# Lightning attention and a mixture of experts on one core: q and k turned in token halves on the two row halves of the array

## The chip, the cores and the metric

The kernel runs on one core of a Trainium2 chip. Its matrix engine (TensorE, "PE" in the profile, with the loading of stationary operands shown apart as "PEld") writes to PSUM banks of 128 partitions by 512 fp32 numbers. VectorE (DVE) and ScalarE (ACT) bring the results from there into SBUF, GpSimd (POOL) works on SBUF alone, and SyncE (SP) and ScalarE issue the DMAs. The metric is the device time of one execution in microseconds (us); less is better.

## The reference

Four batches of eight heads, 768 tokens and 64 numbers per head go through a decayed linear attention; its output, seen as 3072 tokens of 512, goes through four experts whose results are summed with normalised weights. All data are fp32.

```python
for b in range(nb):                                  # blocks of 64 tokens
    intra = einsum('bhic,bhjc->bhij', qb, kb) * Dmask[None]
    intra = einsum('bhij,bhjd->bhid', intra, vb)
    inter = einsum('bhid,bhde->bhie', qb * lam_pow[None], kv_state)
    out[:, :, sl] = intra + inter
    kv_state = lam_block[None, :, None, None] * kv_state + einsum('bhsd,bhse->bhde', kb * rev_pow[None], vb)
...
for e in range(E):                                   # x: (3072, 512), w1: (4, 512, 1024), w2: (4, 1024, 512)
    h = maximum(x @ w1[e], 0.0)
    out += p[:, e:e + 1] * (h @ w2[e])
```

## The kernel before

The tokens are worked on in three groups of 1024. The attention runs in chunks of 128 tokens rather than 64: eight chunks per group, 24 in all, numbered n. The expert products of a group are done by a seven-product scheme in place of eight (M1 to M7), on two levels, so that the operands are sums and differences of blocks, prepared by GpSimd and VectorE and stored by DMA for later use.

The order of all instructions is written by hand: each engine runs its instructions in the order in which the program issues them, and semaphores make an instruction wait for the data and the buffers of others.

A chunk of attention has three steps.

- `turn(n)` (line 420) brings q and k of the chunk from "tokens on partitions" to "head dimension on partitions". The natural tile `qn` holds, for each of four numbers `ac`, two heads side by side (128 columns). TensorE transposes those 128 x 128 blocks one by one: the block of data is the stationary operand and the identity matrix is the moving one. The four blocks of q fill one PSUM bank (`qp`), the four of k another (`kp`). ScalarE copies each bank as a whole, 128 x 512, to `qT` (line 431) and `kT` (line 432). VectorE then makes `qs`, the decayed q, and GpSimd multiplies `kn` by its decay in place, which has to wait until the transposes of k have read it.
- `scores(n)` (line 443) multiplies kT with qT (line 449): each head lies on 64 partitions, so each of these matmuls uses 64 of the 128 rows of the array, and two heads lie in the two halves. They write to two banks, one for each half.
- `values(n)` (line 461) multiplies the masked scores with v (line 477), adds what comes from the state (line 472), and forms the update of the state (line 485). The matmuls of line 485 have 64 columns of stationary operand and 64 of moving data, and alternate between the two column halves of the array.

One fp32 matmul in the program is two MATMUL instructions in the profile, each with its own LDWEIGHTS; a transpose is one.

The first group's attention (chunks 0 to 7, the loop at line 984) is done at the start, with pieces of the first expert products (line 955) put between its steps; there the banks come from three pairs, `pairs[n % 3]`. The 16 other chunks are spread over the expert products of the groups before them: `attention(g)` (line 504) makes a list of steps, and the main loop (line 1035) takes a step after some of its pieces. The banks are then `s0` and `s1`. Around each step lie matmuls of the first product (line 693) and of the second (line 747), with 128 x 128 stationary blocks and 256 moving columns.

The first product writes in turn to two banks, `g1` and `g3`; ScalarE copies (line 701) or VectorE adds (line 699) each result out before TensorE may write to that bank again.

`load(n)` (line 99) issues the DMAs for q and k (line 110) and v (line 106) on SyncE's queue. The stores of prepared weights (lines 148 to 150) are issued on ScalarE's queue, between its computing instructions.

Of the kernel before, what the change touches and what calls it, by code (L numbers as in the profile page):

```python
# [21 lines left out]
def kernel(  # L22
# [30 lines left out]
    nc = tc.nc  # L53

    B, H, S, D = q.shape
# [3 lines left out]
    C = P  # L59
    NHP = H // 2  # L60
# [21 lines left out]
    half = [slice(0, D), slice(D, P)]  # L82
# [4 lines left out]
    def bank(tag, name):  # L87
        return ps.tile([P, W], FP32, name=name, tag=tag)

    def small(name):  # L90
        return pool.tile([P, W], FP32, name=name, tag="t")

    def tt(eng, o, a, b, op):
        eng.tensor_tensor(out=o, in0=a, in1=b, op=op)  # L94
# [204 lines left out]
    ident = consts.tile([P, P], FP32, name="ident")  # L299
# [41 lines left out]
    for r in range(2):  # L341
        for ac in range(NHP):
            h = 4 * r + ac
            nc.vector.tensor_tensor_scan(
                out=s_decay[:, r, ac], data0=lam_bc[:, h:h + 1].to_broadcast([P, C]), data1=ident[:],
# [10 lines left out]
    while m < C:  # L356
        nc.vector.tensor_tensor(
            out=q_decay[:, :, m:2 * m], in0=q_decay[:, :, 0:m],
# [32 lines left out]
    def hc(t):  # L391
        return t[:].rearrange("p (h c) -> p h c", c=C)
# [21 lines left out]
    def soon(n, *work):  # L414

        background[0:0] = work
        if n < CPG:
            rest(len(work))

    def turn(n, tags):  # L420
        qn, kn = nat.pop((n, "q")), nat[n, "k"]
        qp = bank(tags[0], "qp")
        kp = bank(tags[1], "kp")
        for x, y in ((qp, qn), (kp, kn)):
            for ac in range(NHP):
                nc.tensor.transpose(  # L426
                    out=x[:, ac * C:(ac + 1) * C], in_=y[:, 2 * ac:2 * ac + 2].rearrange("p r d -> p (r d)"),
                    identity=ident[:],
                )
        qT, kT, qs = small("qT"), small("kT"), None  # L430
        nc.scalar.copy(out=qT[:], in_=qp[:])
        nc.scalar.copy(out=kT[:], in_=kp[:])
        if n % NCH:
            qs = small("qs")
            soon(n, lambda: tt(nc.vector, qs[:], qT[:], q_decay[:].rearrange("p h c -> p (h c)"), ALU.mult))
        turned[n] = qT, kT, qs
        if n % NCH < NCH - 1:

            kd = kn.rearrange("p (ac r) d -> p ac r d", r=2)
            by = k_decay.rearrange("p r ac -> p ac r").unsqueeze(3)  # L440
            tt(nc.gpsimd, kd, kd, by.to_broadcast([P, NHP, 2, D]), ALU.mult)
# [62 lines left out]
    def attention(g):  # L504

        steps = []
        early, late = prepare_x(g)
        for n in range(g * CPG, (g + 1) * CPG):
            steps.append(lambda n=n: turn(n, ("s0", "s1")))
            steps.append(lambda n=n: scores(n, ("s0", "s1")))  # L510

            def end(n=n):
                values(n, ("s0", "s1"))
                if n + AHEAD < B * NCH:
                    load(n + AHEAD)
                if n == g * CPG + CPG // 2 - 1:
                    chores.extend(early)
                if n == g * CPG + CPG - 1:
                    chores.extend(late)
            steps.append(end)  # L520
        return steps
# [462 lines left out]
    for i in range(CPG + 2):  # L984
        if i == 4:
            sum_w1(0, "S1", "A21", "A22", ALU.add)
            sum_w1(0, "S3", "A11", "A21", ALU.subtract)
        if i == 5:
            sum_w1(0, "S2", "S1", "A11", ALU.subtract)
            sum_w1(0, "S4", "A12", "S2", ALU.subtract)  # L990
            chores.extend(prepare_w2(0))
        if i > 5:
            pump()
        more = list(between.get(i, ()))
        for f, lag in ((scores, 1), (turn, 0), (values, 2)):
            n = i - lag
            if 0 <= n < CPG:
                f(n, pairs[n % 3])
            if i == 9 and lag == 2:
                x_sums()  # L1000
            if more:
                more.pop(0)()
        if i + 4 < CPG:
            load(i + 4)
        if i == 5:
            nc.scalar.dma_start(out=probs[:], in_=moe_domain_probs.rearrange("(t p) e -> p t e", p=P))
        if i == 9:
            gates()
# [26 lines left out]
    for at, (g, e) in enumerate(units):  # L1035
# [14 lines left out]
        for i in range(7):  # L1050
# [7 lines left out]
            if nests and i == 2:  # L1058
                nc.scalar.dma_start(
                    out=gate_bc[:], in_=gate_rows[:, ahead[1]].partition_broadcast(P),  # L1060
# [20 lines left out]
            for x, part in enumerate(order):  # L1081
# [12 lines left out]
                if turned_back and x > 0:  # L1094
                    y = turned_back.pop(0)
# [40 lines left out]
```

## Time and profile before

| | |
|---|---|
| median of 4 runs | 1220.06 us (1217.4 to 1221.35) |
| the profiled execution, its own time | 1220.19 us |
| its span in the profile | 1218.4 us |
| mean granted TensorE clock | 0.997 |
| transposes of line 426 | 96 for q and 96 for k |
| copies of lines 431 and 432 | 24 of 583 ns mean and 24 of 592 ns mean |
| HBM traffic | 233.49 MB read, 85.34 MB written |

The span runs from the first to the last instruction in the profile; 1.8 us of the execution's own time lie around it. In a row of the timeline the columns are the start in us, the length in us, the engine, the line, the operation, and what is written from what; shapes are given as stationary rows*columns, then the moving operand, and "x8" says that eight instructions in a row were merged. Matmuls overlap in the pipeline, so the pace of TensorE is read from start to start and not from the lengths.

### The profile page before, as it was taken

How to read it: one execution, taken by the hardware profiler on the slowest of the kernel's cores; microseconds unless marked ns; L12 is line 12 of the kernel's file. 1: busy time of each engine (PE TensorE's matmuls, PEld its weight loads, DVE VectorE, ACT ScalarE, POOL GpSimd, SP SyncE). 2: the span in 40 equal slices, each digit the busy share in tenths (PEclk: the TensorE clock that was granted, in tenths of full speed). 3: DMA queues.
4: the chain of work that ended last, by engine and by line, in shares of the span. 5: the costliest groups of instructions: out<-in, count | busy, mean ns of one | idle time of the engine just before them, and what ended most of it. 6: DMA issues, size and time to landing. Idle time of an engine off the chain costs nothing.

```text
span 1218.4 us, 17839 instructions
## 1 busy us (share of the span) xinstructions
PE 1194.1 (98%) x6621; PEld 1031.6 (85%) x6621; DVE 780.8 (64%) x1292; ACT 260.5 (21%) x476; POOL 627.1 (51%) x552
## 2 busy tenths in 40 slices
PE   6999998999999999999999999999999999999998
PEld 5888887888888888888888888888888888888877
DVE  5586575477466846746674874774665666777774
ACT  3322121112202211221221120120142241231132
POOL 3520265572382865025425746405675674873873
PEclk9999999999999999999999999999999999999999
DMA  9752679999899699889967999958966657565542
GB/s 227 194 170 108 215 264 336 343 345 316 303 340 341 231 326 368 265 274 293 312 224 266 287 336 351 306 220 299 347 252 220 250 194 275 194 259 210 205 171 72
DMA packets 228534, 320.03 MB, mean 263 GB/s; under 512 B 91712, under 2 KB 168928, under 8 KB 228448
## 3 DMA queue, kind: packets, MB, share of 16 engines
q1 hardware_dynamic: 157984, 233.47, 57.5%
q10 hardware_dynamic: 70464, 85.42, 19.5%
q8 instruction: 52, 0.85, 0.3%
q14 instruction: 34, 0.28, 0.1%
HBM read 233.49 MB, written 85.34 MB: 262 GB/s over the span
## 4 chain that ended last, share of the span: by engine, by line
PE 91%; DVE 3%; DMA 2%; SPq 2%; POOL 1%; issue 1%; ACT 0%; ACTq 0%; POOLq 0%; DVEq 0%
PE pg L693 34%; PE q L747 29%; PE pq L918 13%; PE pM L955 7%; PE op L477 2%; PE sp L449 2%; DVE hS L94 1%; POOL ops L94 1%; PE op L472 1%; DMA w_ops<-ops 1%; SPq L110 1%; DMA w2t<-w_sums 1%; PE qp L426 1%; PE kp L426 1%; DVE m L94 1%; PE op L485 1%
## 5 line engine op out<-in xcount | busy, mean ns | idle before, releaser
L693 PE MATMUL pg<-xs_in,ws_in 128*128 128x256 f32 x1960 | 475.3, 383 | 6.3 <-ACT m L701 4.4
L693 PEld LDWEIGHTS pg<-xs_in,ws_in 128*128 128x128 f32 x1960 | 368.6, 190 | 65.3 <-DVE m L94 8.1
L94 DVE TENSOR_TENSOR m<-pg,m 128x512 f32<-128x512 f32 x410 | 280.3, 689 | 130.2 <-PE pg L693 113.4
L747 PE MATMUL q<-w2t,hS 128*128 128x256 f32 x1024 | 242.5, 380 | 0.0
L747 PEld LDWEIGHTS q<-w2t,hS 128*128 128x128 f32 x1024 | 193.9, 190 | 26.7
L763 DVE SCALAR_TENSOR_TENSOR acc<-q,gate,acc 128x256 f32<-128x256 f32 x192 | 92.6, 482 | 152.8 <-PE q L747 152.5
L747 PE MATMUL q<-w2t,m 128*128 128x256 f32 x768 | 182.6, 381 | 0.0
L747 PEld LDWEIGHTS q<-w2t,m 128*128 128x128 f32 x768 | 146.2, 191 | 20.4
L705 ACT ACTIVATE m<-m 128x512 f32<-128x512 f32 x120 | 74.9, 629 | 320.8 <-DVE m L94 237.9
L94 POOL TENSOR_TENSOR m<-m,gate_bc 128x512 f32<-128x512 f32 x64 | 81.2, 1286 | 61.9 <-ACT m L705 43.4
L94 DVE TENSOR_TENSOR sums<-pq,sums 128x256 f32<-128x256 f32 x154 | 64.6, 422 | 46.8 <-PE pq L918 41.9
L918 PE MATMUL pq<-acc,w2t 128*128 128x256 f32 x352 | 86.6, 379 | 0.0
L94 POOL TENSOR_TENSOR kn<-kn,s_decay 128x512 f32<-128x512 f32 x20 | 22.8, 1141 | 120.5 <-PE kp L426 83.0
L94 POOL TENSOR_TENSOR ops<-w2b 128x256 f32<-128x256 f32 x24 | 17.9, 768 | 125.6 <-DMA w2b<-in_moe_w_dram 107.2
L94 DVE TENSOR_TENSOR m<-m,m 128x512 f32<-128x512 f32 x96 | 80.4, 846 | 0.0
L94 POOL TENSOR_TENSOR w2o<-w2b 128x1024 f32<-128x1024 f32 x16 | 38.5, 2410 | 74.9 <-DMA w2b<-in_moe_w_dram 32.9
L918 PEld LDWEIGHTS pq<-acc,w2t 128*128 128x128 f32 x352 | 66.7, 190 | 9.6 <-issue 0.6
L701 ACT COPY m<-pg 128x512 f32<-128x512 f32 x80 | 46.2, 586 | 130.2 <-PE pg L693 108.4
L642 ACT ACTIVATE m<-m 128x512 f32<-128x512 f32 x48 | 30.3, 630 | 145.3 <-DVE m L94 132.4
L94 POOL TENSOR_TENSOR acc<-hT,hT 128x512 f32<-128x512 f32 x32 | 40.2, 1270 | 33.5 <-PE pq L918 21.5
L94 DVE TENSOR_TENSOR hS<-m,m 128x512 f32<-128x512 f32 x64 | 48.2, 759 | 5.6 <-ACT m L705 5.6
L955 PE MATMUL pM<-xt,w1o 128*128 128x256 f32 x192 | 44.0, 381 | 0.6 <-DVE m L94 0.4
(109 smaller groups left out, 1346.0 us busy)
## 6 DMA issues: line engine op xcount, KB each, us to landing
xs_in<-x_ops SPq DMA_DIRECT2D x70, 896.0 KB, 5.1
ws_in<-w_ops SPq DMA_DIRECT2D x70, 896.0 KB, 7.4
w2t<-w_ops SPq DMA_DIRECT2D x66, 256.0 KB, 6.6
w2t<-w_sums SPq DMA_DIRECT2D x64, 256.0 KB, 5.8
w_ops<-ops ACTq DMA_DIRECT2D x28, 512.0 KB, 7.3
w2t<-in_moe_w_dram SPq DMA_DIRECT2D x48, 256.0 KB, 5.1
x_ops<-ops ACTq DMA_DIRECT2D x21, 512.0 KB, 5.3
w2b<-in_moe_w_dram SPq DMA_DIRECT2D x32, 256.0 KB, 5.1
```

What stands on the lines that cost most here:

```text
L94: eng.tensor_tensor(out=o, in0=a, in1=b, op=op)
L426: nc.tensor.transpose(out=x[:, ac * C:(ac + 1) * C], in_=y[:, 2 * ac:2 * ac + 2].rearrange("p r d -> p (r d)"), identity=ident[:],)
L449: nc.tensor.matmul(out=sp[r][:, ac * C:(ac + 1) * C], lhsT=hc(kT)[half[r], ac], rhs=hc(qT)[half[r], ac], start=True, stop=True,)
L477: nc.tensor.matmul(out=op[r][half[x], a * C:(a + 1) * C], lhsT=vn[:, 4 * r + 2 * a + x], rhs=hc(st[r])[:, 2 * a + x], start=(first and a = ...
L642: nc.scalar.activation(out=o[:], in_=o[:], func=AF.Relu)
L693: nc.tensor.matmul(out=p[:, j * 256:(j + 1) * 256], lhsT=ws[:, W1_AT[i], j * P:(j + 1) * P], rhs=xs[:, X_AT[i]], start=(fresh and j == 0), ...
L701: nc.scalar.copy(out=new[at][:], in_=p[:])
L705: nc.scalar.activation(out=new[at][:], in_=new[at][:], func=AF.Relu)
L747: nc.tensor.matmul(out=p[:, s * DH:(s + 1) * DH], lhsT=h[A_OF[m]][:, c * 256 + s * P:c * 256 + (s + 1) * P], rhs=fed2[g, e, m][uu][:, c], ...
L763: nc.vector.scalar_tensor_tensor(out=o, in0=x, scalar=w, in1=o, op0=ALU.mult, op1=ALU.add)
L918: nc.tensor.matmul(out=p[:, 0:256], lhsT=fed3[e, m, x // 2][:, x % 2, c * P:(c + 1) * P], rhs=b[B_OF[i]][:, c * 256:(c + 1) * 256], start= ...
L955: nc.tensor.matmul(out=p[:, s * 256:(s + 1) * 256], lhsT=a[c][:, f:f + P], rhs=b[:, c, j * 256:(j + 1) * 256], start=(s == 0 and c == 0), ...
```

## The change

In `turn`, each 128 x 128 transpose becomes two transposes of 64 tokens: the stationary operand is the block's upper or lower 64 partitions (64 rows by 128 columns), and the moving operand is the 64 x 64 corner of the identity on the same partitions. The two halves of a block follow each other directly, so that successive instructions use different row halves of the array.

The banks are divided in another way. Before, one bank held q and one held k. Now `tp[0]` holds the first 64 tokens of both q and k, and `tp[1]` the last 64 tokens of both; within a bank the first 256 columns are q and the last 256 are k. A copy therefore has to put 64-token pieces into every 128-token slot of `qT` or `kT`: four copies of 128 x 256 replace the two of 128 x 512.

```diff
     def turn(n, tags):
         qn, kn = nat.pop((n, "q")), nat[n, "k"]
-        qp = bank(tags[0], "qp")
-        kp = bank(tags[1], "kp")
-        for x, y in ((qp, qn), (kp, kn)):
+
+        tp = [bank(tags[t], "tp") for t in range(2)]
+        qT, kT, qs = small("qT"), small("kT"), None
+        for x, y in enumerate((qn, kn)):
             for ac in range(NHP):
-                nc.tensor.transpose(
-                    out=x[:, ac * C:(ac + 1) * C], in_=y[:, 2 * ac:2 * ac + 2].rearrange("p r d -> p (r d)"),
-                    identity=ident[:],
+                for t in range(2):
+                    nc.tensor.transpose(
+                        out=tp[t][:, (x * NHP + ac) * D:(x * NHP + ac + 1) * D],
+                        in_=y[half[t], 2 * ac:2 * ac + 2].rearrange("p r d -> p (r d)"),
+                        identity=ident[half[t], half[t]],
+                    )
+        for x, y in enumerate((qT, kT)):
+            for t in range(2):
+                nc.scalar.copy(
+                    out=hc(y)[:, :, half[t]],
+                    in_=tp[t][:, x * NHP * D:(x + 1) * NHP * D].rearrange("p (h d) -> p h d", d=D),
                 )
-        qT, kT, qs = small("qT"), small("kT"), None
-        nc.scalar.copy(out=qT[:], in_=qp[:])
-        nc.scalar.copy(out=kT[:], in_=kp[:])
```

`half` is `[slice(0, 64), slice(64, 128)]`, and `hc` views a 128 x 512 tile as 128 x 4 x 128.

## The prediction

> **What bounds the kernel now.** I read the page first: how busy each engine is, and which engine holds the chain that ended last.
>
> ```profile
> PE 1194.1 (98%) x6621; PEld 1031.6 (85%) x6621; DVE 780.8 (64%) x1292; ACT 260.5 (21%) x476; POOL 627.1 (51%) x552
> ...
> PE 91%; DVE 3%; DMA 2%; SPq 2%; POOL 1%; issue 1%; ACT 0%; ACTq 0%; POOLq 0%; DVEq 0%
> ```
>
> TensorE is the bound for nearly the whole span, and ScalarE holds none of the chain. So a change in `turn` is worth what it takes from or adds to TensorE's own sequence. Second, the timeline of TensorE around one turn, one score step and one value step in the later groups:
>
> ```profile
> 217.80 0.63 PE L485 MATMUL op<-vn,kn 128*64 128x64 f32 x16
> 218.36 1.13 PE L693 MATMUL pg<-xs_in,ws_in 128*128 128x256 f32 x4
> ...
> 226.24 0.60 PE L426 MATMUL qp<-ident,qn 128*128 128x128 f32 x4
> 226.67 0.60 PE L426 MATMUL kp<-ident,kn 128*128 128x128 f32 x4
> 227.11 1.89 PE L747 MATMUL q<-w2t,m 128*128 128x256 f32 x8
> 228.84 1.89 PE L693 MATMUL pg<-xs_in,ws_in 128*128 128x256 f32 x8
> 230.56 1.89 PE L747 MATMUL q<-w2t,m 128*128 128x256 f32 x8
> 232.38 1.16 PE L449 MATMUL sp<-qT,kT 64*128 64x128 f32 x16
> 233.48 1.13 PE L693 MATMUL pg<-xs_in,ws_in 128*128 128x256 f32 x4
> ```
>
> Starts give the pace: eight large matmuls take 228.84 - 227.11 = 1.73 us, 216 ns each. A turn takes 227.11 - 226.24 = 0.87 us, 109 ns for each of eight transposes; the trace has this value for all 16 turns of the later groups. The score step takes 1.10 us, and starts 0.09 late (230.56 + 1.73 = 232.29, but 232.38 is seen).
>
> Third, the views by tile, for the loads (minimum, median, maximum in ns) and the copies:
>
> ```profile
> L426 PEld LDWEIGHTS qp<-ident,qn x96: 138/141/230, 4.5 to 647.0; 128*128 128x128 f32 x96
> ...
> L449 PEld LDWEIGHTS sp<-qT,kT x384: 182/188/335, 7.4 to 653.7; 64*128 64x128 f32 x192
> ...
> L485 PEld LDWEIGHTS op<-vn,kn x320: 137/138/138, 14.6 to 638.7; 128*64 128x64 f32 x160
> ...
> L490 ACT COPY xT<-op x48: 352/372/381, 14.7 to 668.9; 128x256 f32<-128x256 f32 x48
> ```
>
> A transpose's load of 128 columns (141) costs what line 485's load of 64 columns does (138), not what a score matmul's 128 columns do (188).
>
> **TensorE, one later turn.** Eight transposes of 0.109 go; 16 come, in eight pairs, one in each row half. The trace has no transpose on half of the rows, so I bound it by neighbours. The nearest in time per load and in moving columns is line 485: 64 moving columns, a 138 ns load, pairs alternating between two halves (of columns, though). Its 16 instructions take 218.36 - 217.80 = 0.56. In the trace's single starts the partners start 7 ns apart and the pairs 59 ns, so 8 x 0.059 = 0.47, and the last pair's successor comes 0.10 later than a pair would: leaving the layout. Line 485 pays no entry, because line 477 before it has the same layout. A turn between large matmuls does: 0.09, as the score step shows. After an entry the second pair is also late by its load: in the score step 0.10 (213 ns against 112), at line 472, with 64-column loads, 0.05 (160 ns against 110). I take 0.05, by the length of the load. Together 0.09 + 0.05 + 0.47 + 0.10 = 0.71, against 0.87: 0.16 less.
>
> The bounds: were only the 0.43 of streaming left (8 x 107 ns x 64/128), 0.44 would go. At the pace of the score step, whose stationary operand has just the shape of the new ones, a turn costs 0.09 + 1.10 = 1.19, 0.32 more. With no overlap, 16 x 0.109 and 0.29 for entry, load and exit make 2.03, 1.16 more. I choose 0.71, since the load's length and the 64 moving columns both speak for line 485. Break-even is a pair of (0.87 - 0.24) / 8 = 79 ns.
>
> [...] The score step shows 0.09 in and 0.10 out. [...] Line 485 shows 16 matmuls in 0.56, 35 ns each. [...]
>
> **Over the span.** The later groups have 16 turns: 16 x 0.16 = 2.6 us less. Of the first group, turns 0 to 3 end before this wait:
>
> ```profile
> 25.73 0.63 PE L426 MATMUL qp<-ident,qn 128*128 128x128 f32 x4 [3.14 <-DMA qn<-in_q_dram]
> ```
>
> Until then the chain runs along SyncE's issues and the load of q for turn 4, which wait for none of this. What turns 0 to 3 gain or lose is hidden by those 3.14 us of idle; turns 0 and 1, where the scores wait for kT, become later by some 0.6 each (four copies of 0.37, begun when all transposes are done, against a qT copy that overlapped k's transposes). If that cover were gone, 1.2 us would be paid. In turn 4, k's transposes wait for their own load until 26.63, so only 0.07 goes. Turn 5 (33.92) saves 0.16. Turns 6 and 7 run straight into line 472 and take 0.97 to its start, so they save 0.26 each. Together 0.75.
>
> **ScalarE.** Two copies of 583 and 592 ns (1.18) go, four like line 490's come: 4 x 0.372 = 1.49, so 0.31 more per turn, 7.5 us over 24. I assume that 64-column runs in the output cost nothing; no row shows it. A new wait comes with it: each bank now holds q and k, so I take q's copies to start only when k's transposes into the bank are done too, about 0.3 later in the turn than now. ScalarE is idle 79% of the time, which hides this. What is late next: kT comes about 0.6 later. In the later groups the scores come two or more pieces of 1.73 after the turn. In turn 6, kT was ready at 43.44 and the scores start at 44.68; 1.24 of slack covers it. Behind the copies in ScalarE's queue stands the eviction of the next first-product result (line 701). After a turn, `g1` is wanted again 0.86 + 1.73 = 2.6 later; the copies end at about 1.7 and the eviction at 2.3, so 0.3 is left, and only M1 and M5 evict on ScalarE. If it failed, a few tenths would be lost a handful of times. VectorE's `qs` waits for qT, but is issued behind the next part's work; GpSimd's `kn` product is released 0.1 to 0.2 earlier. Both banks are now needed at the turn's start; their last reader is long done (in the later groups a value step ends some 8 us before the next turn: 218.36 to 226.24). No DMA is added or moved.
>
> **What does not reach the end.** One stall is not TensorE's own:
>
> ```profile
> 199.51 9.49 DMA w_ops<-ops
> ...
> 210.03 3.78 PE pg L693 x8
> ```
>
> These rows of the chain of waits follow a run of GpSimd work from 182.78 on; an ACT copy stood behind a store's issue. TensorE waits 4.39 us here, and its granted clock is then 0.5 for 6.8 us. Arriving earlier only lengthens the wait. I write off the two turns shortly before it (132.6 and 179.1), 0.3.
>
> **Sum.** -2.6 - 0.75 + 0.3 = -3.0 us against the profiled execution's 1220.19 (span 1218.4 and 1.8 around it): 1217.2. The median shown is 1220.06, so the base is 0.1 high at most.
>
> **Rivals.** (1) *The row halves run at the score step's pace.* If the load of a 64-row block lasts as in line 449, or the two transposes don't overlap fully, each later turn costs 1.19, and the first group's turns 5 to 7 cost 0.32, 0.22 and 0.22 more: 16 x 0.32 + 0.8 = 5.9, so 1226.1. It decides from 79 ns per pair on. For it: the operand shape, and that no transpose on half of the rows is in the trace. Against it: the 141 ns load of a transpose, and 64 moving columns instead of 128. (2) *The gain is swallowed.* TensorE is earlier, but waits that are pinned by DMA, GpSimd and VectorE grow: at 205.3, and two on VectorE at 415.2 (1.8 us from start to start) and 717.0 (0.8). If the first takes all of phase one and the others half of the rest, about 1 us is left: 1219.2. For it: the DMA share is 0.92 between 225 and 415. Against it: TensorE has no gap in that stretch (190.0 of 190.0 us busy), so nothing is pinned there. (3) *It doesn't do what it says*: the halves go one after the other. 20 x 1.16 = 23 more, 1243. Against it: lines 449 and 485 both start their partners 7 ns apart.
>
> **How the numbers follow.** Forecast 0.60 (1215 to 1219.5), rival 1 0.23, rival 2 0.13, rival 3 0.04. The range 1213.5 to 1227 takes the forecast with stalls that shift by a few us, rival 2 and rival 1, and leaves out rival 3 and what lies beyond. A measurement tells about 0.2% (2.4 us) from no change, so the border to "faster" is 1217.6, close to my time: of the forecast 0.42 falls beyond it, 0.15 within, 0.03 is turned by a new stall; rival 2 adds 0.09 to the same and the rest of it, 0.04, goes with rivals 1 and 3 to slower, where a stall grows beyond the gain.
>
> **What would show it.** A later turn that starts 0.09 late and takes 0.62 from its first start to the next large matmul's; pairs 59 ns apart, partners 7; loads near 140 ns; four copies near 372 ns; ACT busy at 268. Turns above 0.87 make the prediction wrong in sign; turns at 0.71 with an unchanged total mean rival 2, and the gaps at 205, 415 and 717 would have grown.

## The result, and the profile after

The changed kernel is slower by a little: 1221.92 us median of 48 runs against 1218.98 of 73 of the kernel before, a ratio of 1.0023 [1.0016, 1.003], some 2.8 us. The time lies in the range, and the sign is the wrong one. The profiled execution took 1221.81 us with a span of 1220.0; that of before (1220.19) had been 1.2 us above its own median, so the two profiles show less of the difference than the medians do.

The page of the changed kernel, busy time of the engines and their shares of the chain that ended last:

```profile
PE 1193.6 (98%) x6813; PEld 1026.1 (84%) x6813; DVE 780.1 (64%) x1292; ACT 263.7 (22%) x524; POOL 627.5 (51%) x552
...
PE 86%; DVE 4%; DMA 4%; POOL 3%; SPq 1%; issue 1%; ACT 0%; POOLq 0%; ACTq 0%; DVEq 0%
```

TensorE's busy time fell by 0.5 us only, and its share of the chain by 5 points. Next the same stretch of the timeline of TensorE that the prediction showed, one turn of the later groups (every line after `turn` has moved by six: 753 is the old 747, 699 the old 693, 961 the old 955):

```profile
225.17 1.99 PE L699 MATMUL pg<-xs_in,ws_in 128*128 128x256 f32 x8
227.10 0.46 PE L428 MATMUL tp<-ident,qn 64*128 64x64 f32 x8
227.39 0.41 PE L428 MATMUL tp<-ident,kn 64*128 64x64 f32 x8
227.74 1.99 PE L753 MATMUL q<-w2t,m 128*128 128x256 f32 x8
229.57 1.89 PE L699 MATMUL pg<-xs_in,ws_in 128*128 128x256 f32 x8
```

The turn takes 227.74 - 227.10 = 0.64 from its first start, and begins 0.09 late: 0.73 for the 0.87 of before. In the single starts the two row halves begin 3 to 4 ns apart and the pairs 62 ns. But look at the piece behind it: its eight large matmuls take 229.57 - 227.74 = 1.83, and the eight after these 1.72 (the next piece starts at 231.29). The second matmul after the turn is 0.10 late, which the first start after the turn does not show.

By tile, minimum, median and maximum in ns:

```profile
L428 PEld LDWEIGHTS tp<-ident,qn x192: 134/139/227, 4.5 to 647.6; 64*128 64x128 f32 x192
L428 PE MATMUL tp<-ident,qn x192: 216/223/363, 4.5 to 647.6; 64*128 64x64 f32 x192
...
L435 ACT COPY qT<-tp x48: 353/374/379, 6.7 to 648.4; 128x256 f32<-128x256 f32 x48
L435 ACT COPY kT<-tp x48: 385/394/406, 7.3 to 648.9; 128x256 f32<-128x256 f32 x48
```

The loads and the copies are what the prediction took them for. The copies overlap, though, as the timeline of ScalarE at the same turn shows:

```profile
227.90 0.37 ACT L435 COPY qT<-tp 128x256 f32<-128x256 f32 x1 [0.97 <-PE tp L428]
...
228.16 0.38 ACT L435 COPY qT<-tp 128x256 f32<-128x256 f32 x1
228.43 0.67 ACT L435 COPY kT<-tp 128x256 f32<-128x256 f32 x2
```

From 227.90 to 229.10 the four take 1.20, where the two of before took 1.07 (226.93 to 228.00).

Now the first group, TensorE again, of the changed kernel:

```profile
22.15 1.99 PE L961 MATMUL pM<-xT,w1b 128*128 128x256 f32 x8
26.09 0.46 PE L428 MATMUL tp<-ident,qn 64*128 64x64 f32 x8 [1.95 <-DMA qn<-in_q_dram]
26.95 0.69 PE L428 MATMUL tp<-ident,kn 64*128 64x64 f32 x8 [0.39 <-DMA kn<-in_k_dram]
27.57 3.35 PE L961 MATMUL pM<-xT,w1b 128*128 128x256 f32 x8
...
35.96 0.47 PE L428 MATMUL tp<-ident,qn 64*128 64x64 f32 x8
```

The kernel before, behind the start of its turn 4 at 25.73:

```profile
27.09 1.89 PE L955 MATMUL pM<-xT,w1b 128*128 128x256 f32 x8
...
33.92 0.60 PE L426 MATMUL qp<-ident,qn 128*128 128x128 f32 x4
```

Turn 4 starts 0.37 later than before. But the large matmuls behind it take 3.35 us in place of 1.89, and turn 5 comes 35.96 - 26.09 = 9.87 later, where it came 33.92 - 25.73 = 8.19 later before: 1.68 us more. The windows of the same stretch, of the changed kernel; the columns are the bounds, the length, the busy time of each engine, and the granted clock:

```profile
core 0: us, PE busy (x) PEld busy (x) DVE busy (x) ACT busy (x) POOL busy (x), PEclk, DMA share, GB/s
23.50:26.90 3.40, 1.11 (x11) 0.57 (x10) 0.04 (x1) 0.58 (x1) 2.36 (x2) 1.00 0.95 220
26.95:30.36 3.41, 3.41 (x15) 2.75 (x16) 1.68 (x1) 1.20 (x4) 3.41 (x4) 0.50 1.00 223
```

and of the kernel before:

```profile
24.20:27.60 3.40, 1.60 (x11) 1.37 (x12) 0.59 (x1) 0.84 (x2) 3.40 (x3) 1.00 0.97 220
...
27.60:31.00 3.40, 3.40 (x56) 2.73 (x54) 2.04 (x2) 1.29 (x3) 3.40 (x4) 1.00 1.05 237
```

TensorE waits for the loads of turn 4 in both. In the changed kernel the clock is 0.50 for the 3.41 us that follow (the large matmuls start 427 ns apart there, and 216 ns at full clock), which costs half of these, 1.7 us; before it stays at 1.00 although the idle stretch was longer (3.14 against 1.95 and 0.39). The mean granted clock differs from execution to execution (0.993 to 1.000 in those of the changed kernel), so it has to be read over all runs. With c the mean granted clock of a run, (1 - c) x span is the time lost at half speed. (The start, before the clock first rises, isn't in it. The half clock behind TensorE's last work is, and costs no time: in the profile of the changed kernel that work ends at 1216.2, and the clock is 0.50 for the last 1.8 us, from 1218.2 on.) Over its runs the kernel before loses 1.5 to 2.2 us in the five comparisons below, and the changed one 4.1 (49 runs); in those 49 the time and the mean clock go together with a correlation of -0.74. Over the 134 runs of the kernel before in these comparisons (mean loss 1.8) the time grows by 1.03 us with each us lost, so the count is a fair price. By it some 2.3 of the 2.8 us are lost to the clock.

Where in a run they are lost, the mean doesn't say. The profile of the kernel before has one half clock, 3.4 us lost at the stall behind 205 (208.5 to 215.3). That of the changed kernel has two, 1.7 lost behind turn 4 and 1.7 at that stall (211.3 to 214.7). So these two profiles lose about as much as each other, and that the surplus of the many runs arises at turn 4 is for the experiments to show.

### The profile page after: what moved, and what is told of

It is laid out like the page before. It is cut to its first block, busy times and chain, and to the rows that moved or that the text cites. A ratio compares the mean times of both kernels' runs of the same rounds, so it can differ in the third digit from the quotient of the medians.

```text
span 1220.0 us, 18273 instructions
## 1 busy us (share of the span) xinstructions
PE 1193.6 (98%) x6813; PEld 1026.1 (84%) x6813; DVE 780.1 (64%) x1292; ACT 263.7 (22%) x524; POOL 627.5 (51%) x552
## 4 chain that ended last, share of the span: by engine, by line
PE 86%; DVE 4%; DMA 4%; POOL 3%; SPq 1%; issue 1%; ACT 0%; POOLq 0%; ACTq 0%; DVEq 0%
PE pg L699 34%; PE q L753 27%; PE pq L924 13%; PE pM L961 5%; PE op L483 2%; PE sp L455 2%; DVE m L94 2%; POOL ops L94 2%; DVE hS L94 1%; PE tp L428 1%; PE op L478 1%; DMA w2b<-in_moe_w_dram 1%; POOL w1o L94 1%; DMA w1b<-in_moe_w_dram 1%; SPq L110 1%; DMA w_ops<-ops 1%
## 5 line engine op out<-in xcount | busy, mean ns | idle before, releaser
L699 PEld LDWEIGHTS pg<-xs_in,ws_in 128*128 128x128 f32 x1960 | 368.5, 190 | 66.7 <-DVE m L94 10.3
L753 PEld LDWEIGHTS q<-w2t,hS 128*128 128x128 f32 x1024 | 193.9, 190 | 26.8
```

The costliest lines, as they stand in the source:

```text
L699: nc.tensor.matmul(out=p[:, j * 256:(j + 1) * 256], lhsT=ws[:, W1_AT[i], j * P:(j + 1) * P], rhs=xs[:, X_AT[i]], start=(fresh and j == 0), ...
L753: nc.tensor.matmul(out=p[:, s * DH:(s + 1) * DH], lhsT=h[A_OF[m]][:, c * 256 + s * P:c * 256 + (s + 1) * P], rhs=fed2[g, e, m][uu][:, c], ...
```

## The experiments

Each ratio is against runs of the kernel before in the same comparison. The last columns are the us lost at half clock, mean over all runs, of the experiment and of the kernel before beside it.

| run | ratio [95%] | median us, before's | lost | before's |
|---|---|---|---|---|
| e1_late_new | 0.9991 [0.9982, 1.0001] | 1217.41, 1217.63 | 1.00 | 1.65 |
| e2_first_new | 1.0008 [0.9995, 1.0022] | 1219.47, 1217.63 | 3.45 | 1.65 |
| e3_warm | 1.0024 [1.0009, 1.0038] | 1221.16, 1217.63 | 3.46 | 1.65 |
| e4_copies | 1.0038 [1.0023, 1.0054] | 1222.61, 1217.63 | 2.89 | 1.65 |
| e6_warm14 | 1.0029 [1.0015, 1.0042] | 1220.20, 1218.40 | 3.66 | 1.47 |
| e7_after | 1.0052 [1.0039, 1.0066] | 1224.10, 1218.40 | 3.91 | 1.47 |
| e8_delay | 1.0103 [1.0088, 1.0118] | 1229.02, 1218.40 | 5.16 | 1.47 |
| e10_late_warm | 1.0013 [1.0001, 1.0026] | 1219.93, 1218.40 | 1.44 | 1.47 |
| e11_turn4_old | 1.0017 [0.9996, 1.0039] | 1220.71, 1218.17 | 3.15 | 1.85 |
| e12_turn4_new | 1.0018 [1.0002, 1.0034] | 1220.83, 1218.17 | 2.54 | 1.85 |
| e13_delay2 | 1.0020 [1.0006, 1.0034] | 1219.80, 1218.17 | 0.81 | 1.85 |
| e14_from5_new | 1.0012 [0.9987, 1.0038] | 1217.73, 1218.17 | 1.84 | 1.85 |
| e15_reload_old | 0.9994 [0.9976, 1.0012] | 1217.46, 1218.32 | 2.03 | 1.80 |
| e16_reload_new | 0.9987 [0.9974, 1.0001] | 1217.24, 1218.32 | 1.01 | 1.80 |
| e17_reload2_new | 0.9988 [0.9974, 1.0001] | 1217.56, 1218.92 | 1.42 | 2.17 |
| e18_reload2_old | 0.9989 [0.9973, 1.0006] | 1217.57, 1218.92 | 1.93 | 2.17 |

**Which turns lose.** My theory (A below) was that the first group loses through its clock and that the 16 later turns gain a little; the rivals were that the later turns lose, and that the copies do. Two kernels divide the turns:

```diff
     def turn(n, tags):
+        if n >= CPG:
+            tp = [bank(tags[t], "tp") for t in range(2)]
...
+        else:
+            qp = bank(tags[0], "qp")
```

This is e1: the old way in turns 0 to 7, the new one in the 16 later turns.

> The first eight turns as before, the 16 later ones as changed. Theory A (the loss arises in the first group: kT comes later in turns 0 and 1, TensorE is less busy there, and its clock is granted late): each later turn costs 0.09 late start + 0.64 + 0.10 late second matmul behind it = 0.83 against 0.87, so 16 x 0.04 = 0.6 us less than before, ratio 0.9990 to 1.0000; the start at 25.7 of turn 4 and the clock from about 10.5 us as before. Theory B (the loss arises in the later groups, by ScalarE's longer copies or by stalls that shift): ratio 1.0015 to 1.0035, like the changed kernel.

It is not slower, and its interval just reaches 1: the later turns do not lose. One thing in it was not expected: its clock first rises at 16.8, and not at about 10.5 as in the profile of before. The changed kernel's rises at 16.7, and this late rise had been part of theory A. But e15, with old turns, rises at 17.2, and e17, with new ones, at 11.0, so the first rise doesn't tell the two forms apart. e2 has `n < CPG`, the new way in the first group alone.

> The first eight turns as changed, the 16 later ones as before. Theory A: the whole loss and none of the later gain, ratio 1.0020 to 1.0035; full clock only from about 17 us, turn 5 at about 36.0 instead of 33.9. Theory B: ratio 0.999 to 1.0005.

Its 1.0008 is less than expected and the interval holds 1. Its profile has the half clock from 27.2 to 30.6 and turn 5 at 9.8 us after turn 4, as the changed kernel has, and its lost time is the changed kernel's kind, 3.45. But e1 and e2 together make less than the whole change does.

**The copies alone.** e4 keeps the old transposes and makes four copies of them:

```diff
-        nc.scalar.copy(out=qT[:], in_=qp[:])
-        nc.scalar.copy(out=kT[:], in_=kp[:])
+        for x, y in ((qT, qp), (kT, kp)):
+            for t in range(2):
+                nc.scalar.copy(out=hc(x)[:, :, half[t]], in_=hc(y)[:, :, half[t]])
```

> Transposes as before, but each bank copied in two halves of 64 tokens per head, four copies of 128x256 per turn. Theory A: kT is later by some 0.3 in turns 0 and 1, TensorE's work is as before, so the clock is granted nearly as before (10.5 to 14 us) and the 3.1 us of wait at 25.7 take up the rest: ratio 0.9995 to 1.0010. Theory B with ScalarE's copies as the cause: ratio 1.0015 to 1.0035.

This missed: it is 1.0038. Its timeline shows one of the places where it loses:

```profile
318.81 4.66 POOL L94 TENSOR_TENSOR w2o<-w2b 128x1024 f32<-128x1024 f32 x2 [32.36 <-DMA w2b<-in_moe_w_dram]
...
321.19 0.33 ACTq L221 DMA_DIRECT2D w_sums<-w2o  x1
321.61 0.65 ACT L433 COPY qT<-qp 128x256 f32<-128x256 f32 x2 [7.96 <-POOL w2o L94]
...
322.67 0.63 ACT L702 COPY m<-pg 128x512 f32<-128x512 f32 x1
323.35 1.59 PEld L694 LDWEIGHTS pg<-xs_in,ws_in 128*128 128x128 f32 x8 [1.22 <-ACT m L702]
323.35 1.99 PE L694 MATMUL pg<-xs_in,ws_in 128*128 128x256 f32 x8 [0.82 <-ACT m L702]
```

ScalarE stood 7.96 us behind a store's issue (ACTq) that waited for GpSimd; the copies queue behind it, the eviction of line 702 behind the copies, and TensorE waits for that. This is the queue that the prediction named (the eviction behind the copies), though the 1.2 us here are mostly the store's wait and not the copies' length. Other stalls, not behind these copies, stand at 353 (1.0) and 867 (2.3); the last is also in e8 (878) and e15 (863), which have the old copies. The profile of the changed kernel doesn't have the ones at 322 and 353, so they don't explain it. What makes e4 as slow as it is was not followed further. That four copies as such are not the changed kernel's loss is seen below: e16 and e17 make them in all 24 turns and are not slower than the kernel before.

**Filling the wait.** If TensorE only has to be kept busy, matmuls that nobody reads would keep the clock. e3 is the changed kernel with such matmuls of the identity: 7 ahead of turn 0, 3 behind turns 0 and 1, 6 ahead of turn 4. e6 has 14 ahead of turn 4.

```diff
+    def warm(times):
+        w = bank("g3", "wm")
+        for _ in range(times):
+            nc.tensor.matmul(out=w[:, 0:C], lhsT=ident[:], rhs=ident[:], start=True, stop=True)
...
+                if f is turn and n == 4:
+                    warm(6)
```

> The changed kernel with 19 matmuls of the identity with itself added in the first group, into a bank that nobody reads: 7 before the first turn, 3 after each of turns 0 and 1, 6 before turn 4, all at places where TensorE waits. Theory A with the clock as its main part: full clock from 7 to 10 us, no half clock around 27, turn 5 at 33.6 to 34.2, ratio 0.9985 to 1.0005. If the later kT and not the clock is the main part: full clock as early, but turn 5 still at 35 to 36, ratio 1.0015 to 1.003. Theory B: ratio 1.0015 to 1.003 with turn 5 at 34.

> As the run with matmuls of the identity put into TensorE's waits, but 14 of them (3.0 us) instead of 6 before turn 4, so that they fill the wait for its data. Theory C: no half clock near 27 us, turn 5 about 8.1 us after turn 4 instead of 9.9, the time lost to half clock 1 to 2.5 us instead of 3.5, ratio 0.9990 to 1.0010. Theory D (late kT and ScalarE's longer copies cost the time, the clock only follows): no half clock near 27 either, but ratio 1.0015 to 1.003.

e3's clock rose earlier, at 9.7, and still fell from 26.8 to 30.2: 6 matmuls are too few, and the ratio did not move. In the profile of e6 the clock holds, and what the half clock costs is then plain to see:

```profile
21.66 3.29 PE L423 MATMUL wm<-ident 128*128 128x128 f32 x28
25.48 0.46 PE L433 MATMUL tp<-ident,qn 64*128 64x64 f32 x8 [0.53 <-DMA qn<-in_q_dram]
26.28 0.46 PE L433 MATMUL tp<-ident,kn 64*128 64x64 f32 x8 [0.34 <-DMA kn<-in_k_dram]
26.67 1.99 PE L966 MATMUL pM<-xT,w1b 128*128 128x256 f32 x8
...
33.70 0.46 PE L433 MATMUL tp<-ident,qn 64*128 64x64 f32 x8
```

Turn 5 comes 33.70 - 25.48 = 8.22 after turn 4 (9.87 in the changed kernel), and the span is 1213.8. Yet over its runs e6 was at 1.0029 and lost 3.66 us to the clock, so other runs of it lost the clock somewhere. Where, the one profile can't show. In the same comparison the changed kernel was run again, unaltered:

> The changed kernel again, beside the others of this call. Theory C (the loss is TensorE's clock: after the wait for turn 4 the shorter transposes leave TensorE too idle, it gets half the clock for 3.4 us from about 27 us on, which costs 1.7; the later stall at 205 to 211 follows): ratio 1.0015 to 1.003, time lost to half clock (1 minus the mean granted clock, times the span) about 4 us against 1.6 of the kernel before, and a half clock near 27 us in the profile.

Its 1.0052 lies above what was expected and is from five runs, and its profile has the half clock from 25.5 to 32.3, two such steps. Last, e10 gives e1 the matmuls of e6.

> The first eight turns as before, the later 16 as changed, and the same 27 matmuls of the identity in TensorE's waits of the first group. Theory C: no half clock in the first group, 0.6 us from the later turns, ratio 0.9985 to 0.9998. Theory D: the same, since the first group's turns are the old ones; a ratio above 1.001 would speak against both.

It missed too, at 1.0013. It lost no more clock than the kernel before (1.44), but its profile has stalls at 144 (1.7), 161 (1.1) and 207 (3.0). Whatever the filling gains in the first group is not seen in the time. The one at 144, a wait for VectorE, stands in both profiles of the changed kernel too (1.2 and 1.4 us), and not in that of before. It is no rival for the whole loss, as e16 and e17 below have it and are not slower.

**Does lateness reach the end?** The prediction wrote off part of a gain at the stall at 205, and it let four turns be late for nothing. e8 and e13 put eight matmuls into the old kernel behind the first group, in the bank "g3" and in "q11".

```diff
+    w = bank("q11", "wm")
+    for _ in range(8):
+        nc.tensor.matmul(out=w[:, 0:C], lhsT=ident[:], rhs=ident[:], start=True, stop=True)
```

> The kernel before with eight matmuls of the identity (1.7 us) put behind the first group's attention, at about 58 us: TensorE is late by what the half clock costs, and nothing else changes. If lateness goes through to the end: ratio 1.0010 to 1.0018. If stalls pinned by DMA and GpSimd at 205 take it up: 0.9995 to 1.0008. If a late TensorE makes the stall at 205 longer: 1.0025 or more.

> The delay at 58 us again, with a bank that has long been free: eight matmuls of the identity, 1.7 us and no wait. If lateness goes through to the end: ratio 1.0010 to 1.0018, and no half clock at 66 us. If the later stalls take it up: 0.9995 to 1.0008.

e8 doesn't do what was meant: the bank was still in use, and its timeline shows not a delay of 1.7 us but a wait:

```profile
60.50 1.99 PE L955 MATMUL pM<-xT,w1b 128*128 128x256 f32 x8
66.76 1.65 PE L1013 MATMUL wm<-ident 128*128 128x128 f32 x6 [4.27 <-DVE m L94]
```

A half clock goes with it (65.9 to 72.8). TensorE is 2.7 us behind the profile of before at 60.5 and 10.3 behind it at 70.3; over the runs e8 ends 10.6 later. e13 puts in what was meant:

```profile
56.50 1.99 PE L955 MATMUL pM<-xT,w1b 128*128 128x256 f32 x8
58.34 1.95 PE L1013 MATMUL wm<-ident 128*128 128x128 f32 x16
60.12 4.05 PE L955 MATMUL pM<-xt,w1o 128*128 128x256 f32 x18
```

Some 1.8 us go in. The starts of the two pieces around it are 3.62 apart where they were 2.22 before, so 1.4 us are net, and 1.0020 [1.0006, 1.0034], 2.4 us and at least 0.7, come out at the end. What TensorE loses early is paid at the end. What it gains early need not arrive there: in the profiles of e17 and e18 below, e17 is 2.9 us ahead at turn 7 (43.00 against 45.87) and ends 1.4 behind (spans 1216.0 and 1214.6), as it loses 3.4 us to the clock at the stall behind 205 and e18 loses 1.7.

**Is it turn 4?** e11 is the changed kernel with turn 4 the old way (`if n != 4`), e12 the old kernel with turn 4 alone the new way (`if n == 4`), and e14 takes the new way from turn 5 on (`if n >= 5`).

> The changed kernel with turn 4 alone, the one that waits for its load at 25.7, in the old form. Theory C (TensorE is too idle around turn 4 and gets half the clock for 3.4 us or more, which makes the first group late by 1.7): the half clock behind turn 4 becomes rarer, since the old turn keeps TensorE busy for 0.9 us on all rows, turn 5 mostly 8.2 us after turn 4, time lost to half clock 1.5 to 2.5 us, ratio 0.9995 to 1.0015. Theory D (late kT and ScalarE's copies in the whole first group): ratio 1.002 to 1.004, like the changed kernel.

> The kernel before with turn 4 alone in the new form: one turn of 24. Theory C: half clock behind turn 4, turn 5 9.8 us after it, time lost to half clock 2.5 to 4 us, ratio 1.0010 to 1.0025. Theory D: no change to be told, 0.999 to 1.0007.

> Turns 0 to 4 as before, turns 5 to 23 as changed: what theory C would choose. Turns 5 to 7 save 0.5 us together, the 16 later ones 0.04 each, 0.6: ratio 0.9985 to 0.9998. Theory D: about half of the first group's loss is left, 1.0005 to 1.002.

Both e11 and e12 come out near 1.0017, between the kernel before and the changed one, and e11's interval holds 1. So turn 4 does not look like the whole of it, with the new way or without. With turn 4 old, e11 still loses 3.15 us to the clock, more than the 1.5 to 2.5 expected, and its profile shows no half clock, so where is not seen. e14 is too wide to tell by its time, with a median just under that of before; it loses no more clock than before does (1.84, but that scatters by 2.4 from run to run), so nothing says that the new turns 5 to 7 cost the clock. In e12's profile, by windows, the clock is lost ahead of its changed turn, which starts at 25.76:

```profile
core 0: us, PE busy (x) PEld busy (x) DVE busy (x) ACT busy (x) POOL busy (x), PEclk, DMA share, GB/s
21.70:25.10 3.40, 1.22 (x6) 0.73 (x4) 0.61 (x2) 0.58 (x1) 0.91 (x1) 1.00 1.02 293
```

The clock is half from 25.1 on. Until then this kernel executes just what the kernel before does, so its profile says nothing of the new turn: here the wait alone, with 1.22 us of TensorE in 3.40, cost the clock. What turn 4 adds to that can only be seen over many runs, and there (2.54 against 1.85) it is small and within the scatter (0.7, give or take 1.0).

**The wait taken away.** What remained open was whether the new turns cost something themselves, or only through the wait at turn 4. One theory (C) says that without the wait the new turns are as good as the old ones, or better; its rival (D), that they stay behind by two or three us. e15 and e16 load v of turn 3 and q and k of turn 4 earlier in SyncE's queue, v ahead of one block of weights and q and k ahead of three (A12, A21, A22); e15 has the old turns, e16 the new.

```diff
-    raw_w1(0, "A12")
     load(3, "v")
+    load(4, "qk")
+    raw_w1(0, "A12")
     raw_w1(0, "A21")
...
-            load(i + 4)
+            load(i + 4, "v" if i == 0 else "qkv")
```

> The kernel before, with the loads of q and k of chunk 4 issued before w1's blocks A12, A21 and A22 instead of behind them. Both theories: the wait of 3.1 us in front of turn 4 shrinks to under 1 us, turn 4 at 22.5 to 24; ratio 0.997 to 1.000, if the later stalls don't take it up.

> The changed kernel with the same order of loads. Theory C: no half clock near 25 to 30 us, time lost to half clock as in its sister with the old turns within 0.8 us, and the two ratios within 0.001 of each other (the new turns up to 1.1 us faster). Theory D: 0.002 to 0.003 above its sister, with turns 5 to 7 later than there by 0.5 us or more though the clock is whole.

The timeline of e16 around turn 4:

```profile
19.91 1.99 PE L962 MATMUL pM<-xT,w1b 128*128 128x256 f32 x8
21.83 0.46 PE L429 MATMUL tp<-ident,qn 64*128 64x64 f32 x8
22.13 0.41 PE L429 MATMUL tp<-ident,kn 64*128 64x64 f32 x8
22.47 1.99 PE L962 MATMUL pM<-xT,w1b 128*128 128x256 f32 x8
...
30.36 0.46 PE L429 MATMUL tp<-ident,qn 64*128 64x64 f32 x8 [0.79 <-DMA qn<-in_q_dram]
31.90 0.46 PE L429 MATMUL tp<-ident,kn 64*128 64x64 f32 x8 [1.08 <-DMA kn<-in_k_dram]
```

No wait and no half clock at turn 4; turn 5 now waits for its loads, 0.8 and 1.1. In e15 turn 4 has no wait either, but comes only at 25.20, not at 22.5 to 24, behind that late first rise of its clock. e17 and e18 bring the q and k of turn 5 forward too, e17 with the new turns and e18 with the old. Against e16, e17 changes:

```diff
     load(4, "qk")
     raw_w1(0, "A12")
+    load(5, "qk")
     raw_w1(0, "A21")
...
-            load(i + 4, "v" if i == 0 else "qkv")
+            load(i + 4, "v" if i < 2 else "qkv")
```

> The changed kernel with q and k of chunks 4 and 5 loaded before w1's blocks A21 and A22 (chunk 4 before A12 too). Theory C: no wait over 1 us for turns 4 and 5, no half clock in the first group, turn 6 at 38 to 40, ratio 0.9965 to 0.9990, within 0.001 of its sister with the old turns. Theory D: 0.002 or more above its sister.

> The kernel before with the same order of loads. Both theories: no wait over 1 us for turns 4 and 5, turn 6 at 38 to 41, ratio 0.9970 to 1.0000.

With the wait gone, new and old turns cannot be told apart: 0.9987 and 0.9994, 0.9988 and 0.9989, all intervals over one another. The new turns lose 1.01 and 1.42 us to the clock there, no more than the old ones (2.03 and 1.93), where the changed kernel loses 4.1. Taken together, the new turns are 0.2 us faster than the old ones, give or take 1.2. So the rival falls, at the size of two or three us that it named: without the wait for turn 4's loads the loss is gone. A cost of up to 1 us is not excluded. All four medians lie about 1 us below that of before, but each interval reaches 1 (e16 to 1.0001), so no version is shown to beat both kernels; against the changed kernel, these are 3.5 to 4.4 us better, by the ratios (0.9987 to 0.9994 against 1.0023, times 1219).

## Why the prediction was wrong

That the time lies in the range is luck: the range reached up to 1227 for rival 1, which did not come true. Right were the mechanism inside the turn and its prices. The row halves overlap (62 ns per pair for the 59 foretold), the loads take 139 ns, the entry costs 0.09, and the turn to the next large matmul's start takes 0.73 for 0.71. Rivals 1 and 3 fall with that. Scores 0 and 1 are later by 0.58 and 0.49 (7.40 to 7.98, 11.70 to 12.19), for the 0.6 foretold. The last piece ahead of the wait began 1.56 late (22.15 for 20.59; the clock's later first rise is in that too), and the wait took most of it up: turn 4 started 0.37 late.

Wrong in size was the term of 0.10 for leaving the layout. Leaving the layout costs 0.10 ahead of the next large matmul and another 0.10 ahead of the second one, whose load starts 0.106 behind the first one's start (227.843, 227.737), where behind the other large matmuls there it is 0.001 to 0.003. The entry was given its late second pair, and the exit was not. The profile of before had it, behind a score step:

```profile
193.92 1.16 PE L449 MATMUL sp<-qT,kT 64*128 64x128 f32 x16
195.02 1.99 PE L955 MATMUL pM<-xt,w1b 128*128 128x256 f32 x8
196.85 1.89 PE L747 MATMUL q<-w2t,hS 128*128 128x256 f32 x8
```

The eight behind the score step take 1.83 with 1.99 on the line, the others 1.73 with 1.89. So it was behind line 485, from which the term came: the large matmuls there start at 218.361, 218.681 and 218.897, and so 0.10 late a second time. A later turn thus saves 0.87 - 0.73 - 0.10 = 0.04 and not 0.16, and 16 of them 0.6 us and not 2.6. The starts agree: in the two profiles the changed kernel is 1.04 us behind at turn 12 and 0.63 at turn 23, 0.04 less with each turn. (At turn 9 it was 2.64 behind; the stall behind 205, which was longer in the profile of before, took 1.8 of that back.) What e1 measured (0.9991, -1.1 us, between -2.2 and +0.1) holds the 0.6; the 2.6 lies outside.

Wrong in kind was the step "what turns 0 to 3 gain or lose is hidden by those 3.14 us of idle". The start of turn 4 is hidden, as it said. But the wait was no free cover: in more of the profiles than with the old turns the new first group comes out of it at half clock (0.50 from 26.95 to 30.36 in that of the changed kernel), and then 1.7 us are lost behind it, and a loss of that kind reaches the end (e13). The prediction saw such a price at 205, "its granted clock is then 0.5 for 6.8 us", and didn't ask about it at the other long wait. Half clock near turn 4 stands in all five profiles in which turn 4 is new and the wait not filled or too little (the changed kernel twice, e2, e3, e12), in one of the seven in which turn 4 is old (e8, but not before, e1, e4, e11, e13, e14), and in none of the four without the wait. That is a hint and no proof, since e12's clock fell ahead of its new turn. The means over all runs (4.1 us lost for 1.8) and e15 to e18 carry the reading: the loss goes for the most part through the clock, and it needs the wait. How the new turns bring it about is argued from single profiles and not shown, and e6, which filled the wait and did not get the time back, speaks against the simplest form of it.

The 0.75 for the first group's turns 4 to 7 went the same way as the 2.6: in the profiles turns 5, 6 and 7 save 0.03, 0.22 and 0.24 for the foretold 0.16, 0.26 and 0.26, and one loss of clock takes 1.7.

The term for ScalarE, "0.31 more per turn", was too large: successive copies overlap, and the four take 0.13 longer than the two did. As it was hidden either way, nothing hung on it. Rival 2, the swallowed gain, came nearer in time (1219.2) but has the wrong cause: there was little gain to swallow, and the stall at 205 did not grow (4.0 us from start to start against 4.8). The wait at 415 kept its 1.8; that at 717 went from 0.8 to 1.4, but it has 1.8 in e12 and e13, whose later turns are old.

Open remain: how the loss divides between turn 4 and the other turns of the first group (e11 and e12 each lie between the two kernels, with wide intervals), why e1 and e2 together lose less than the whole change, where e11 and the changed kernel lose the clock in runs without a profile, why e6 lost the clock over its runs and not in its profile, and what the later stalls of e4 and e10 come from.

## What to carry to other kernels

Where a step changes the array's layout, price the way out by the starts of two instructions behind it, not one: here the second was as late as the first, 0.10 us each, and that took most of the gain. A wait of the bound engine that hides a small loss may have a price of its own, here 1.7 us behind the wait at turn 4: ask what the clock does behind it, and read that over all runs, since one profile shows one draw. On a kernel with such a wait, a change of a few tenths of a percent may be decided there. Moving the loads that cause it did away with the difference here; filling it with idle matmuls did not.

## What the runs showed of the hardware

The length of a gap did not decide over the clock here. The kernel before kept it through 3.14 us of idle, and the changed kernel lost it with 1.95 and 0.39. What goes with it in the two kernels' profiles is how much TensorE does in the 3.41 us ahead. From one change of the clock to the next these traces have 3.413, 6.827, 10.24, 180.9, 198.0 and 1003.5 us, all multiples of 3.413. Cut into steps of that length, back from the half clocks, TensorE is busy for 0.56 us in the step ahead of the half clock of before (205.08 to 208.49), and for 1.08 (23.53 to 26.95) and 0.30 (207.85 to 211.27) ahead of the two of the changed kernel; at the ends, where the clock falls too, it is 0.00 and 0.77. Of the steps at full clock behind which the clock held, the least busy has 1.58 (24.17 to 27.58, the wait at turn 4 of before). In the other profiles the 3.40 us ahead of a loss have 1.09 (e3), 1.22 (e12), 1.31 (the changed kernel again), and 1.34 and 0.00 (e8, ahead of 28.4 and 65.9). e2 doesn't fit, as it lost the clock after 1.89; why, no run shows. Where the half clock begins differs from execution to execution (with the new turn 4 at 26.95, 27.20, 26.75, 25.11 or 25.47). That the same wait is cut at another place each time, and leaves another amount of work in the step, is an estimate from these starts.

Two matmuls on different row halves, of 64 rows each, start 3 to 4 ns apart, each with a load of its own of 139 ns, so at the pace of 62 ns per pair 16 half transposes take 0.50 where eight whole ones take 0.87. Besides that, at the turn at 227.10 this layout costs 0.09 to enter, 0.05 on the second pair (111 ns for 62), and 0.20 to leave, half of it at the second large matmul (320 ns for 216).

Copies out of a bank overlap on ScalarE: in the changed kernel they take 0.37 us and start 0.26 apart (227.90, 228.16). The prediction's sum of single copies left these 0.11 us out.
